# RWKV attention with a two-layer MLP: new planner costs, new load order, no 4-byte loads, filler matmuls

## The chip, the cores and the metric

One core of one Trainium2 chip runs the kernel. The metric is the device time in microseconds (us); the median of the runs is compared.

## What is computed

```python
def _attn_ref(r, k, v, w, u):          # r, k, v: (4, 8, 768, 48); w, u: (8, 48)
    for t in range(S):
        cur = np.einsum('bhd,bhe->bhde', u[None] * kt, vt)
        y[:, :, t] = np.einsum('bhd,bhde->bhe', rt, state + cur)
        state = w[None, :, :, None] * state + np.einsum('bhd,bhe->bhde', kt, vt)

def _moe_ref(x, w_in, w_out):          # x: (3072, 384); d_ff 2048
    h = x @ w_in
    g = np.where(h >= 1, h, np.where(h <= -1, 0.0, (h + 1) ** 2 / 4))
    return g @ w_out                   # x is y with heads and head_dim side by side
```

## The kernel before

The sequence is cut into 6 chunks of 128 steps. Batch b and chunk c make one of 24 **units** (4 batches inside each chunk, so units 0 to 3 have no earlier state). Two units make one of 12 **blocks** of 256 tokens for the MLP.

Attention of a unit: load K, R, V (192 KB each, `add_load`); scale K by `Winv` and R by `Wpow` into a bf16 tile `KR` (`kw`, `rw`); cast V (`v`); transpose `KR` into `RK`; multiply pairs of heads into scores (`at`, L429), mask them into `AT` on DVE (`mask`, L435); read out with `AT` and the state `Tbd` into y (`y`, L485 and L488); add the diagonal term `VD` (`x`, L500); transpose x into `xT`; update the state (`st` on PE L536, `t`, `tw`, `bd`). Units 0 to 7 are **soft**: transposes go through PE (`tr` L409, `xp` L510) and the diagonal through PE (`dg` L451). Units 8 to 23 are hard: both transposes are DMAs on SP's queue (L418, L518) and the diagonal is made by POOL (`ku` L464 and L465, `vd` L475) and DVE.

MLP of a block: 8 groups of layer 1 (`h`, L574: 6 matmuls of 256 columns each), a square on ACT after each (`g`, L586), then 8 groups of layer 2 (`o`, L597: 4 matmuls of 384 columns; 4 groups for each unit), a copy of PSUM (`os`, L242) and a store (`out`, L611). Group n of layer 1 needs quarter n//2 of `w_in`; group s of layer 2 needs quarter s of `w_out`. All eight quarters (768 KB, "I0" to "I3" and "O0" to "O3") are loaded as float32 and cast by ACT, DVE or POOL.

Order of the work. `Plan.run` is a list scheduler in Python that runs when the kernel is built: it keeps a model time for each engine, takes the ready operation with the smallest `due`, picks its engine from the costs (`pe`, `act`, `dve`, `pool`), and writes the result out as fixed in-order queues for the engines. MLP groups are due at 1000 and up, so any ready attention operation goes ahead of them. A DMA's model is a begin at least 0.3 us behind its issue, a given length, and 1.7 us until it counts as landed. `D_m` holds the blocks' due times, `ORDER` the order of the first loads. All loads, stores and DMA transposes stand in SP's one queue; the loads of `w` and `u` stand in ACT's: `w_bc`, `u_bc` and four loads of single 4-byte words into `wraw` and `uraw` (`tiny`), from which `wc` (the decay of a chunk) and `uw` are made.

Of the kernel before, what the change touches and what calls it, by code (L numbers as in the profile page):

```python
# [8 lines left out]
F32 = mybir.dt.float32  # L9
# [116 lines left out]
def pe(t):  # L126
    return {"PE": (t, t + 0.17)}
# [22 lines left out]
def kernel(  # L150
# [11 lines left out]
    nc = tc.nc  # L162
# [16 lines left out]
    NS = 8  # L179
# [12 lines left out]
    P = Plan(slots)  # L192

# [11 lines left out]
    def row_bcast(src):  # L205
        return bass.AP(tensor=src.tensor, offset=src.offset, ap=[[0, 128], [1, H * D]])
# [3 lines left out]
    wraw = const.tile([128, NP], F32, name="wraw")  # L210
    uraw = const.tile([128, NP], F32, name="uraw")
# [36 lines left out]
    def tiny(dst, src):  # L248
        with nc.allow_non_contiguous_dma(reason="384 words"):
# [3 lines left out]
    c_wbc = P.op("c_wbc", {"ACT": (0.6, 2.5)}, lambda e: nc.scalar.dma_start(out=w_bc, in_=row_bcast(w)), due=-100)  # L253
# [7 lines left out]
    kr0 = [P.op(f"c_kr{i}", {"DVE": (0.35, 0.4)}, f_kr(i), due=-90 + i if i < 2 else 0) for i in range(slots["KR"])]  # L261

# [3 lines left out]
    c_icol = P.op("c_icol", {"DVE": (0.3, 0.35)}, f_col, deps=[c_cols], due=-99)  # L266
# [14 lines left out]
    c_wu0 = P.op("c_wu0", {"DVE": (0.3, 0.3)}, f_wu, due=-95)

    def f_wu1(e):
        tiny(wraw, w)
        tiny(uraw, u)
    c_wu = P.op("c_wu", {"ACT": (1.8, 4.0)}, f_wu1, deps=[c_wu0], due=-99)
    c_ubc = P.op("c_ubc", {"ACT": (0.6, 4.5)}, lambda e: nc.scalar.dma_start(out=u_bc, in_=row_bcast(u)), due=-94)
# [54 lines left out]
    w_in_ready = {}  # L342
    w_out_ready = {}
    for q in range(NQ):
        bf = Buf("wf")

        def fn(e, bf=bf, q=q):
            t = get(bf, [128, nKb, FQ], F32)
            nc.sync.dma_start(out=t, in_=w_in_src[:, :, q * FQ : (q + 1) * FQ])

        o = P.op(f"ldI{q}", {"SP": (0.2, 0)}, fn, allocs=[bf], due=-200.0 + pos[f"I{q}"], dma=2.05)
        lst = []
        for kk in range(nKb):
            def fc(e, bf=bf, q=q, kk=kk):
                copy(e, w_in_sb[:, kk, q * FQ : (q + 1) * FQ], bf.t[:, kk, :])
            lst.append(P.op(f"cI{q}{kk}", {**dve(FQ, True), **act(FQ, False), **pool(FQ, False)}, fc, deps=[o], uses=[bf], due=D_m[0] + 1.3 * q))
        w_in_ready[q] = lst
    for q in range(NQ):
        bf = Buf("wf")

        def fn(e, bf=bf, q=q):
            t = get(bf, [128, TQ, d_out], F32)
            nc.sync.dma_start(out=t, in_=w_out_src[:, q * TQ : (q + 1) * TQ, :])

        o = P.op(f"ldO{q}", {"SP": (0.2, 0)}, fn, allocs=[bf], due=-200.0 + pos[f"O{q}"], dma=2.05)
        lst = []
        for i in range(TQ):
            def fc(e, bf=bf, q=q, i=i):
                copy(e, w_out_sb[:, q * TQ + i, :], bf.t[:, i, :])
            lst.append(P.op(f"cO{q}{i}", {**dve(d_out, True), **act(d_out, False), **pool(d_out, False)}, fc, deps=[o], uses=[bf], due=34.0 + 1.0 * q))  # L370
        w_out_ready[q] = lst
# [6 lines left out]
    def attention(i):  # L378
# [16 lines left out]
        o_rw = P.op(f"rw{i}", both, f_rw, deps=[Ro, c_wpow, o_kw], uses=[Rb, krb], due=D0 - 5.8)  # L395
# [4 lines left out]
        o_v = P.op(f"v{i}", {**dve(384, True), **act(384, False), **pool(384, False)}, f_v, deps=[Vo], uses=[Vb], allocs=[vb], due=D0 - 4)  # L400
# [14 lines left out]
        else:  # L415
# [3 lines left out]
            o_rk = P.op(f"trd{i}", {"SP": (1.7, 0)}, f_trd, deps=[o_kw, o_rw], uses=[krb], allocs=[rkb], due=D0 - 9, dma=1.4)  # L419
# [109 lines left out]
        if c < NCH - 1:  # L529
# [203 lines left out]
```

## Time and profile before

| what | value |
|---|---|
| runs (median of 3) | 194.84 us (194.29 to 196.55) |
| the profiled execution | 196.34 us |
| its span, first to last instruction | 194.4 us |
| PE, DVE, ACT, POOL busy | 164.1, 110.5, 107.9, 106.8 us |
| DMA moved | 31.68 MB |

Times in the rows are counted from the span's start. PE's busy time overlaps: a row of x6 matmuls lasts until its last result is out, while the next row has begun. What a group costs PE in a stream is the distance from its start to the next row's start.

### The profile page before, as it was taken

How to read it: one execution, taken by the hardware profiler on the slowest of the kernel's cores; microseconds unless marked ns; L12 is line 12 of the kernel's file. 1: busy time of each engine (PE TensorE's matmuls, PEld its weight loads, DVE VectorE, ACT ScalarE, POOL GpSimd, SP SyncE). 2: the span in 40 equal slices, each digit the busy share in tenths (PEclk: the TensorE clock that was granted, in tenths of full speed). 3: DMA queues.
4: the chain of work that ended last, by engine and by line, in shares of the span. 5: the costliest groups of instructions: out<-in, count | busy, mean ns of one | idle time of the engine just before them, and what ended most of it. 6: DMA issues, size and time to landing. Idle time of an engine off the chain costs nothing.

```text
span 194.4 us, 4322 instructions
## 1 busy us (share of the span) xinstructions
PE 164.1 (84%) x1642; PEld 121.0 (62%) x1642; DVE 110.5 (57%) x223; ACT 107.9 (55%) x226; POOL 106.8 (55%) x155
## 2 busy tenths in 40 slices
PE   0453984988999997998997989799979999999990
PEld 0242873757777766775774767576757777777650
DVE  4669698799999957675556676586845300000000
ACT  2316573785856582866556665645665455555210
POOL 7336163567799895988769797977963000000000
PEclk9999998599999999999999999999999999999998
DMA  5999999989899968898797988888776211111121
GB/s 93 183 302 233 350 180 249 269 204 235 206 233 150 215 130 186 171 199 166 147 208 154 201 179 153 203 183 181 155 159 193 66 42 40 43 41 40 44 82 51
DMA packets 106747, 31.68 MB, mean 163 GB/s; under 512 B 99808, under 2 KB 105184, under 8 KB 106720
## 3 DMA queue, kind: packets, MB, share of 16 engines
q1 hardware_dynamic: 105600, 30.94, 70.5%
q10 hardware_dynamic: 1120, 0.40, 1.4%
q8 instruction: 15, 0.25, 0.6%
q14 instruction: 12, 0.10, 0.2%
HBM read 20.84 MB, written 4.72 MB: 131 GB/s over the span
## 4 chain that ended last, share of the span: by engine, by line
PE 45%; DMA 20%; DVE 12%; POOL 8%; SPq 6%; ACT 4%; issue 3%; DVEq 0%; POOLq 0%; ACTq 0%
PE h L574 19%; PE o L597 19%; DMA Vf<-in_v_dram 7%; DMA R<-in_r_dram 6%; DVE AT L435 4%; DMA K<-in_k_dram 4%; SPq L326 4%; DMA out_dram<-os 3%; PE a L409 2%; POOL VD L475 2%; POOL KR L394 2%; POOL KU L465 2%; DVE x L500 2%; POOL KU L464 1%; PE a L488 1%
## 5 line engine op out<-in xcount | busy, mean ns | idle before, releaser
L574 PE MATMUL h<-xT,w_in_sb 128*128 128x256 bf16 x576 | 79.6, 277 | 2.4 <-ACT g L586 1.9
L597 PE MATMUL o<-w_out_sb,g 128*128 128x384 bf16 x384 | 75.7, 326 | 1.3 <-DVE os L242 1.3
L586 ACT ACTIVATE g<-h 128x512 bf16<-128x512 f32 x96 | 56.0, 593 | 32.0 <-PE h L574 30.7
L574 PEld LDWEIGHTS <-w_in_sb 128*128 128x128 bf16 x576 | 55.2, 99 | 16.6 <-issue 3.1
L597 PEld LDWEIGHTS <-g 128*128 128x128 bf16 x384 | 35.7, 98 | 17.7 <-issue 1.4
L435 DVE TENSOR_TENSOR AT<-a,umask 128x512 bf16<-128x512 f32 x48 | 30.8, 682 | 6.5 <-PE a L429 6.3
L526 ACT ACTIVATE x<-x 128x384 bf16<-128x384 bf16 x24 | 12.5, 522 | 16.8 <-DVE x L500 16.7
L394 POOL TENSOR_TENSOR KR<-R,Wpow 128x384 bf16<-128x384 f32 x16 | 16.6, 1039 | 6.7 <-DMA R<-in_r_dram 5.5
L500 DVE TENSOR_TENSOR x<-a,VD 128x384 bf16<-128x384 f32 x24 | 13.3, 552 | 8.9 <-PE a L488 8.4
L465 POOL TENSOR_TENSOR KU<-KU,R 128x384 f32<-128x384 f32 x16 | 17.1, 1071 | 1.3
L464 POOL TENSOR_TENSOR KU<-K,u_bc 128x384 f32<-128x384 f32 x16 | 17.2, 1076 | 0.0
L475 POOL TENSOR_TENSOR VD<-V,dg 128x384 f32<-128x384 bf16 x16 | 13.6, 855 | 6.6 <-DVE dg L470 3.2
L390 DVE TENSOR_TENSOR KR<-K,Winv 128x384 bf16<-128x384 f32 x16 | 11.3, 709 | 9.1 <-DMA K<-in_k_dram 6.0
L409 PE MATMUL a<-ident,KR 128*128 128x128 bf16 x64 | 6.9, 264 | 8.0 <-DVE KR L390 6.5
L242 ACT COPY os<-o 128x384 f32<-128x384 f32 x16 | 7.6, 478 | 9.3 <-PE o L597 7.1
L242 ACT CAST V<-Vf 128x384 bf16<-128x384 f32 x15 | 7.6, 508 | 8.4 <-DMA Vf<-in_v_dram 8.3
L543 DVE TENSOR_TENSOR T<-T,a 48x192 f32<-48x192 f32 x32 | 11.1, 347 | 1.0 <-PE a L536 0.6
L429 PE MATMUL a<-RK 48*128 48x128 bf16 x192 | 10.4, 229 | 1.5 <-DVE RK L242 1.1
L536 PE MATMUL a<-V,KR 128*128 128x96 bf16 x80 | 7.3, 219 | 5.0 <-ACT V L242 2.6
L409 PEld LDWEIGHTS <-KR 128*128 128x128 bf16 x64 | 5.3, 118 | 8.9 <-DVE KR L390 6.5
L488 PE MATMUL a<-V,AT 128*128 128x48 bf16 x192 | 9.2, 189 | 1.5 <-DVE VD L457 1.3
L536 PEld LDWEIGHTS <-KR 128*128 128x128 bf16 x80 | 5.6, 105 | 6.6 <-issue 6.2
(70 smaller groups left out, 165.9 us busy)
## 6 DMA issues: line engine op xcount, KB each, us to landing
K<-in_k_dram SPq DMA_DIRECT2D x24, 192.0 KB, 4.3
R<-in_r_dram SPq DMA_DIRECT2D x24, 192.0 KB, 3.8
Vf<-in_v_dram SPq DMA_DIRECT2D x24, 192.0 KB, 4.3
out_dram<-os SPq DMA_DIRECT2D x24, 192.0 KB, 2.3
wf<-in_moe_w_in_dram SPq DMA_DIRECT2D x4, 768.0 KB, 7.0
wf<-in_moe_w_out_dram SPq DMA_DIRECT2D x4, 768.0 KB, 6.0
RK<-KR SPq DMA_TRANSPOSE x16, 3.3
xT<-x SPq DMA_TRANSPOSE x16, 2.4
```

The costliest lines, as they stand in the source:

```text
L242: (nc.scalar.copy if eng == "ACT" else V_ENG[eng].tensor_copy)(o, i)
L394: V_ENG[e].tensor_mul(krb.t[:, :H, 0:D], Rb.t, Wpow)
L409: nc.tensor.transpose(trb.t[:, p, :], pair(krb.t, p), ident)
L435: nc.vector.tensor_mul(atb.t[s], at_p[s].t, umask4)
L464: nc.gpsimd.tensor_mul(kub.t, Kb.t, u3)
L465: nc.gpsimd.tensor_mul(kub.t, kub.t, Rb.t)
L475: nc.gpsimd.tensor_mul(vdb.t, vb.t, dgb.t[:, :, None].to_broadcast([128, H, D]))
L500: nc.vector.tensor_add(xb.t, yb.t[:, 0:384].rearrange("p (h d) -> p h d", h=H), vdb.t)
L536: mm(stb.t[:, p, :], pair(krb.t[:, H:, :], p), pair(vb.t, p), start=True, stop=True)
L574: mm(hb.t[:, f, :], w_in_sb[:, kk, (2 * n + f) * 128 : (2 * n + f + 1) * 128], xT[m][:, kk, :], start=(kk == 0), stop=(kk == nKb - 1),)
L586: nc.scalar.activation(gb[m].t[:, 2 * n : 2 * n + 2, :], hb.t, AF.Square, bias=0.5, scale=0.5)
L597: mm(ob.t, gb[m].t[:, f, j * C : (j + 1) * C], w_out_sb[:, f, :], start=(f == 0), stop=(f == nN - 1))
```

## The change

The planner gets a new DMA model: each DMA has a length, a number of descriptors and a start delay; an issuing queue holds at most 160 descriptors in its ring; only 8 DMAs of SP and ACT are in flight; a DMA counts as landed 0.6 us behind its end (1.6 us after model time 45). After 45 each PE operation of attention is taken to be ready 0.6 us later than its inputs. Due times, the loads' order and the stores' due time change. In hard units `rw` is on DVE alone, `v` on ACT alone, `bd` on ACT alone; in soft units `bd` is on ACT or POOL. The four 4-byte loads go: `wc` and `uw` are made from one row by 8 small transposes on PE. `u_bc` moves from ACT's queue to SP's, behind unit 7. Matmuls of a zero tile into a spare bank fill PE's planned idle time until model time 24; 224 of them are left in the program.

```diff
+CFG = {
+    "order": "U0 U1 U2 U3 I0 I1 I2 I3 O0 O1 U4 O2 O3 U5 U6 U7",
+    "soft": 8, "sw": False, "due": [13.0, 22.0, 30.0, 36.0, 42.0],
+    "step": 12.6, "warm": 24.0, "steady": 45.0,
+}
...
+                if o.dma and "POOL" not in o.engs and len(lanes) >= 8:
+                    ready = max(ready, lanes[-8])
+                if "PE" in o.engs and ready > steady and o.name[0] != "L":
+                    ready += 0.6
+                if o.late is not None and max(free["PE"], ready) > o.late:
+                    gone.append(o)
+                    continue
...
-                issue = est + occ
-                if len(dmas) >= 2:
-                    issue = max(issue, dmas[-2])
-                begin = max(dma_end, issue + 0.3)
-                dma_end = begin + o.dma
-                dmas.append(dma_end)
+                took, nd, wait = o.dma
+                issue, ring = est + occ, rings[e]
+                while sum(n for t, n in ring if t > issue) + nd > 160:
+                    issue = min(t for t, n in ring if t > issue)
+                begin = max(served, issue + wait)
+                served = begin + took
+                ring.append((served, nd))
                 free[e] = issue
-                o.end = dma_end + 1.7
+                o.end = served + 0.6 + (1.0 if est > steady else 0.0)
...
-    def tiny(dst, src):
-            for s in range(2):
-                nc.scalar.dma_start(out=dst[halves[s], :], in_=src.rearrange("(p s) d -> s d p", s=2)[s])
+    c_ur = P.op("c_ur", {"ACT": (0.4, 0)}, lambda e: nc.scalar.dma_start(out=u_row, in_=...), after=[c_wbc], ...)
+    c_ubc = P.op("c_ubc", {"SP": (0.4, 0)}, lambda e: nc.sync.dma_start(out=u_bc, in_=row_bcast(u)), ...)
...
+    def f_z(e):
+        nc.vector.memset(zero, 0.0)
+        nc.vector.memset(ones, 1.0)
+        nc.vector.memset(onef, 1.0)
+        nc.vector.memset(rows, 0.0)
+        nc.vector.memset(uw, 0.0)
...
+    def f_colT(e):
+        get(colb, [128, 2, NP], F32)
+        for i in range(2):
+            for p in range(NP):
+                nc.tensor.transpose(colb.t[:, i, p : p + 1], rows[:, i, 2 * p : 2 * p + 2, :].rearrange("q h d -> q (h d)"), onef)
...
+    for i in range(160):
+        def f_wm(e, i=i):
+            for _ in range(2):
+                mm(wmb.t, zero, zero, start=True, stop=True, skip_group_check=True)
+        wm0 = P.op(f"wm{i}", pe(0.11), f_wm, deps=[c_z], ..., due=2000.0, late=CFG["warm"] if i else None)
...
-    D_m = [13.0, 18.0, 24.0, 30.0, 36.0] + [44.0 + 12.4 * i for i in range(NB)]
...
-        o_rw = P.op(f"rw{i}", both, f_rw, ...)
+        o_rw = P.op(f"rw{i}", both if soft else {"DVE": both["DVE"]}, f_rw, ...)
-        o_v = P.op(f"v{i}", {**dve(384, True), **act(384, False), **pool(384, False)}, f_v, ...)
+        o_v = P.op(f"v{i}", {**act(384, False), **({**dve(384, True), **pool(384, False)} if soft else {})}, f_v, ...)
-            o_bd = P.op(f"bd{i}", {**scaled(act(192, False), 2), **scaled(pool(192, False), 2), **scaled(dve(192, True), 2)}, f_bd, ...)
+            o_bd = P.op(f"bd{i}", {**scaled(act(192, False), 2), **(scaled(pool(192, False), 2) if soft else {})}, f_bd, ...)
-        P.op(f"out{i}", {"SP": (0.4, 0)}, ..., due=lambda ready, last: ready + 2, dma=0.5)
+        P.op(f"out{i}", {"SP": (0.4, 0)}, ..., due=lambda ready, last: oe.end - 12, dma=(0.8, 8, 0.6))
```

SP's queue, the first loads before. `wf` is a quarter of a weight, K, R and Vf one unit each; the rows begin with unit 1.

```order
L326 DMA K_148<-in_k_dram 128x8x48
L326 DMA R_151<-in_r_dram 128x8x48
L326 DMA Vf_154<-in_v_dram 128x8x48
L349 DMA wf_159<-in_moe_w_in_dram 128x3x512
L349 DMA wf_179<-in_moe_w_in_dram 128x3x512
L326 DMA K_188<-in_k_dram 128x8x48
L326 DMA R_215<-in_r_dram 128x8x48
L326 DMA Vf_262<-in_v_dram 128x8x48
L349 DMA wf_273<-in_moe_w_in_dram 128x3x512
L349 DMA wf_282<-in_moe_w_in_dram 128x3x512
L326 DMA K_297<-in_k_dram 128x8x48
```

The same queue now, from unit 3 on.

```order
L366 DMA K_359<-in_k_dram 128x8x48
L366 DMA R_389<-in_r_dram 128x8x48
L366 DMA Vf_424<-in_v_dram 128x8x48
L402 DMA wf_452<-in_moe_w_in_dram 128x3x512
L402 DMA wf_474<-in_moe_w_in_dram 128x3x512
L402 DMA wf_491<-in_moe_w_in_dram 128x3x512
L402 DMA wf_510<-in_moe_w_in_dram 128x3x512
L402 DMA wf_535<-in_moe_w_out_dram 128x4x384
L366 DMA K_554<-in_k_dram 128x8x48
L402 DMA wf_629<-in_moe_w_out_dram 128x4x384
L366 DMA R_676<-in_r_dram 128x8x48
L366 DMA Vf_747<-in_v_dram 128x8x48
```

Before, two quarters came behind unit 1, two behind unit 2, and one behind each of units 4 to 7. Now all of `w_in` and half of `w_out` come between units 3 and 4, and the other two quarters behind unit 4.

PE's queue around its first layer-1 group, before (repeated rows left out; L510 is `xp` of unit 1, L409 `tr` of unit 2):

```order
L510 LDWEIGHTS x_301
L510 MATMUL a_305<-ident,x_301 128x128
L574 LDWEIGHTS w_in_sb
L574 MATMUL h_315<-xT_94,w_in_sb 128x256
L409 LDWEIGHTS KR_84
L409 MATMUL a_327<-ident,KR_84 128x128
```

The same place now (L469 is `at` of unit 3, L338 a filler, L491 `dg` of unit 3):

```order
L469 LDWEIGHTS RK_542
L469 MATMUL a_589<-RK_542 128x128
L338 LDWEIGHTS zero
L338 MATMUL o_131<-zero 128x128
L614 LDWEIGHTS w_in_sb
L614 MATMUL h_620<-xT_96,w_in_sb 128x256
L491 LDWEIGHTS P_601
L491 MATMUL a_631<-uw,P_601 128x2
```

Layer 1 of block 0 stood behind the attention of units 0 and 1; now it stands behind nearly all PE work of units 0 to 3. 96 fillers stand ahead of PE's first transpose, 2 right ahead of it and 126 between later attention operations.

## Rows read from the trace of the kernel before

**Rows 1.** The page: busy time, share and instructions of each engine.

```profile
PE 164.1 (84%) x1642; PEld 121.0 (62%) x1642; DVE 110.5 (57%) x223; ACT 107.9 (55%) x226; POOL 106.8 (55%) x155
```

**Rows 2.** Busy time by stretch (us): columns as the first line says.

```profile
core 0: us, PE busy (x) PEld busy (x) DVE busy (x) ACT busy (x) POOL busy (x), PEclk, DMA share, GB/s
0.00:19.36 19.36, 6.62 (x71) 4.52 (x72) 13.02 (x30) 7.18 (x15) 9.81 (x28) 1.00 0.88 202
19.36:31.59 12.23, 9.60 (x108) 7.83 (x107) 10.24 (x21) 6.44 (x14) 4.83 (x8) 1.00 0.99 266
31.59:39.23 7.64, 6.86 (x71) 5.33 (x71) 5.50 (x12) 5.49 (x11) 3.69 (x6) 0.55 1.01 246
39.23:48.00 8.77, 7.31 (x96) 5.43 (x93) 8.23 (x16) 6.68 (x16) 6.45 (x11) 1.00 0.93 214
48.00:60.00 12.00, 11.52 (x134) 9.09 (x132) 11.23 (x23) 7.81 (x18) 10.62 (x14) 1.00 1.05 226
60.00:150.00 90.00, 82.73 (x886) 60.76 (x885) 60.29 (x119) 55.28 (x121) 71.43 (x92) 1.00 0.86 176
150.00:189.50 39.50, 39.47 (x294) 28.00 (x289) 1.98 (x6) 18.53 (x34) 0.00 (x0) 1.00 0.14 49
```

**Rows 3.** Timeline of PE, 6 to 22 us: start, us, what, idle before.

```profile
6.54 0.61 PE L409 MATMUL a<-ident,KR 128*128 128x128 bf16 x4 [6.54 <-DVE KR L390]
...
19.36 1.44 PE L574 MATMUL h<-xT,w_in_sb 128*128 128x256 bf16 x6 [0.57 <-ACT xT L242]
20.59 1.06 PE L409 MATMUL a<-ident,KR 128*128 128x128 bf16 x8
21.44 0.53 PE L536 MATMUL a<-V,KR 128*128 128x96 bf16 x4
```

**Rows 4.** Timeline of PE, 46 to 51 us.

```profile
46.05 0.82 PE L574 MATMUL h<-xT,w_in_sb 128*128 128x256 bf16 x6
46.80 0.40 PE L429 MATMUL a<-RK 48*128 48x128 bf16 x8
47.13 0.25 PE L451 MATMUL a<-uw,P 128*128 128x2 bf16 x4
47.24 0.81 PE L597 MATMUL o<-w_out_sb,g 128*128 128x384 bf16 x4
47.89 1.47 PE L574 MATMUL h<-xT,w_in_sb 128*128 128x256 bf16 x12
49.20 0.61 PE L409 MATMUL a<-ident,KR 128*128 128x128 bf16 x8
49.65 0.34 PE L485 MATMUL a<-Tbd,RK 128*128 128x96 bf16 x4
49.82 0.36 PE L488 MATMUL a<-V,AT 128*128 128x48 bf16 x8
50.02 0.33 PE L536 MATMUL a<-V,KR 128*128 128x96 bf16 x4
```

**Rows 5.** Timeline of ACT: two operations released by loads.

```profile
12.47 0.51 ACT L242 CAST V<-Vf 128x384 bf16<-128x384 f32 x1 [4.00 <-DMA Vf<-in_v_dram]
...
50.73 0.93 ACT L242 CAST w_out_sb<-wf 128x384 bf16<-128x384 f32 x2 [0.73 <-DMA wf<-in_moe_w_out_dram]
```

**Rows 6.** Waits of SP's queue: who, for whom, us in total, times, longest.

```profile
SPq L611 <- ACT os L242: 34.9, 10, 4.9
...
SPq L326 <- DMA K<-in_k_dram: 1.1, 1, 1.1
```

**Rows 7.** Groups by line, 60 to 150 us.

```profile
L242 ACT CAST Tbd<-T 48x192 bf16<-48x192 f32 x16 | 5.6, 348 | 1.4 <-POOL T L548 1.1
```

**Rows 8.** Timeline of DVE: its zeroing of KR, and what follows it.

```profile
1.40 2.11 DVE L258 MEMSET KR<- 128x512 uint32 x4
5.93 0.56 DVE L390 TENSOR_TENSOR KR<-K,Winv 128x384 bf16<-128x384 f32 x1 [2.42 <-ACT Winv L290]
```

**Rows 9.** Timeline of PE: the last readout of attention (unit 23).

```profile
149.77 0.36 PE L488 MATMUL a<-V,AT 128*128 128x48 bf16 x8
```

More of the change, by code (lines that the diff above doesn't have):

```diff
@@ L15 @@
 SEM = 0.06
+CFG = {
+    "order": "U0 U1 U2 U3 I0 I1 I2 I3 O0 O1 U4 O2 O3 U5 U6 U7",
+    "soft": 8,
+    "sw": False,
+    "due": [13.0, 22.0, 30.0, 36.0, 42.0],
+    "step": 12.6,
+    "warm": 24.0,
+    "steady": 45.0,
+}
 class Buf:
@@ L23, with __init__ @@
 class Op:
-    def __init__(self, name, engs, fn, deps, uses, allocs, due, dma, after, nb):
+    def __init__(self, name, engs, fn, deps, uses, allocs, due, dma, after, nb, late):
         self.name, self.engs, self.fn, self.due, self.dma = name, engs, fn, due, dma
-        self.after, self.nb = [a for a in after if a], nb
+        self.after, self.nb, self.late = [a for a in after if a], nb, late
         self.deps, self.uses, self.allocs = [d for d in deps if d], list(uses), list(allocs)
@@ L66, in run @@
     def run(self):
-        free = dict.fromkeys(("PE", "ACT", "DVE", "POOL", "SP", "ACTQ"), 0.0)
-        dmas, dma_end = [], 0.0
+        free = dict.fromkeys(("PE", "ACT", "DVE", "POOL", "SP"), 0.8)
+        rings = {"SP": [], "ACT": [], "POOL": []}
+        lanes, served = [], 2.1
         todo, done, last_mlp = list(self.ops), [], "L2"
+        steady = CFG["steady"]
         while todo:
-            cand = []
+            cand, gone = [], []
             for o in todo:
                 if any(d.start is None for d in o.deps) or any(a.start is None for a in o.after):
+                    if o.late is not None and free["PE"] > o.late:
+                        gone.append(o)
                     continue
@@ L78, in run @@
                 ready = max([d.end + SEM for d in o.deps] + [a.start + 0.001 for a in o.after] + [pl[0], o.nb])
+                if o.dma and "POOL" not in o.engs and len(lanes) >= 8:
[3 more added lines that the diff above has]
+                if o.late is not None and max(free["PE"], ready) > o.late:
+                    gone.append(o)
+                    continue
                 for e in o.engs:
                     cand.append((max(free[e], ready), ready, o, e, pl[1]))
-            if not cand:
+            for o in gone:
+                todo.remove(o)
+                for b in o.uses:
+                    b.users.remove(o)
+            if not cand and not todo:
+                break
                 raise RuntimeError("no operation can be placed: " + ", ".join(o.name for o in todo[:12]))
@@ L178 @@
     LIM = 0.95
-    NS = 8
+    NS = CFG["soft"]
+    D_m = list(CFG["due"])
+    while len(D_m) < NB + 2:
+        D_m.append(D_m[-1] + CFG["step"])
     mm = nc.tensor.matmul
@@ L192 @@
     P = Plan(slots)
+    rows = rot.tile([1, 2, H, DP], F32, name="rows", tag=f"g_{slots['g'] - 1}")
     def get(b, shape, dtype):
@@ L259, in f_kr @@
         return fn
-    kr0 = [P.op(f"c_kr{i}", {"DVE": (0.35, 0.4)}, f_kr(i), due=-90 + i if i < 2 else 0) for i in range(slots["KR"])]
+    kr0 = [P.op(f"c_kr{i}", {"DVE": (0.48, 0.5)}, f_kr(i), due=-90 + i) for i in range(slots["KR"])]
     def f_col(e):
@@ L275, with f_uw @@
     c_um = P.op("c_um", {"POOL": (0.6, 0.7)}, f_um, due=-97)
-    def f_wu(e):
-        nc.vector.memset(wraw, 1.0)
-        nc.vector.memset(uraw, 1.0)
+    def f_z(e):
+        nc.vector.memset(zero, 0.0)
         nc.vector.memset(ones, 1.0)
[L281 to L287, printed above, removed]
+        nc.vector.memset(onef, 1.0)
+        nc.vector.memset(rows, 0.0)
+        nc.vector.memset(uw, 0.0)
+    c_z = P.op("c_z", {"DVE": (0.5, 0.5)}, f_z, due=-95)
+    c_lrow = P.op("c_lrow", act(384, False), lambda e: nc.scalar.activation(rows[:, 0, :, 0:D], w_bc[0:1].rearrange("p (h d) -> p h d", h=H), AF.Ln), deps=[c_wbc, c_z], due=10)
+    c_urow = P.op("c_urow", dve(384), lambda e: nc.vector.tensor_mul(rows[:, 1, :, 0:D], w_bc[0:1].rearrange("p (h d) -> p h d", h=H), u_row.rearrange("p (h d) -> p h d", h=H)), deps=[c_wbc, c_ur, c_z], due=8.5)
+    colb = Buf("a")
+    def f_colT(e):
[3 more added lines that the diff above has]
+                nc.tensor.transpose(colb.t[:, i, p : p + 1], rows[:, i, 2 * p : 2 * p + 2, :].rearrange("q h d -> q (h d)"), onef)
+    c_colT = P.op("c_colT", pe(0.5), f_colT, deps=[c_lrow, c_urow], allocs=[colb], due=9)
+    c_wc = P.op("c_wc", {"ACT": (0.15, 0.2)}, lambda e: nc.scalar.activation(wc, colb.t[:, 0, :], AF.Exp, scale=float(C)), deps=[c_colT], uses=[colb], due=10)
+    def f_uw(e):
+        for s in range(2):
+            nc.vector.tensor_copy(uw[halves[s], :, s], colb.t[halves[s], 1, :])
+    c_uw = P.op("c_uw", {"DVE": (0.3, 0.35)}, f_uw, deps=[c_colT, c_z], uses=[colb], due=9)
+    wmb = Buf("o")
+    for i in range(160):
+        def f_wm(e, i=i):
+            if wmb.t is None:
+                get(wmb, [128, 128], F32)
+            for _ in range(2):
+                mm(wmb.t, zero, zero, start=True, stop=True, skip_group_check=True)
+        wm0 = P.op(f"wm{i}", pe(0.11), f_wm, deps=[c_z], uses=[wmb] if i else [], allocs=[] if i else [wmb], after=[wm0] if i else [], due=2000.0, late=CFG["warm"] if i else None)
     flat = lambda t: t.rearrange("p h d -> p (h d)")
@@ L343 @@
-    w_out_ready = {}
-    for q in range(NQ):
+    w_in_ready, w_out_ready = {}, {}
+    prev_w = []
+    for tag, q in [(x[0], int(x[1:])) for x in ORDER if x[0] in "IO"]:
         bf = Buf("wf")
[L347 to L371, printed above, removed]
+        if tag == "I":
+            src, dst, shape = w_in_src[:, :, q * FQ : (q + 1) * FQ], w_in_sb[:, :, q * FQ : (q + 1) * FQ], [128, nKb, FQ]
+        else:
+            src, dst, shape = w_out_src[:, q * TQ : (q + 1) * TQ, :], w_out_sb[:, q * TQ : (q + 1) * TQ, :], [128, TQ, d_out]
@@ new lines, with fn, fc @@
+        nd = 24 if tag == "I" else 32
+        res = w_in_ready if tag == "I" else w_out_ready
+        due = -200.0 + pos[f"{tag}{q}"]
+        before = ORDER[: pos[f"{tag}{q}"]]
+        gate = [loads[int(x[1:])]["Vf"][1] for x in before if x[0] == "U"][-1:]
+        if CFG["sw"]:
+            def fn(e, src=src, dst=dst):
+                nc.gpsimd.dma_start(out=dst, in_=src)
+            o = P.op(f"ld{tag}{q}", {"POOL": (1.1, 0)}, fn, after=gate + prev_w[-1:], due=due, dma=(2.05, 0, 1.0))
+            res[q] = [o]
+        else:
+            def fn(e, bf=bf, src=src, shape=shape):
+                t = get(bf, shape, F32)
+                nc.sync.dma_start(out=t, in_=src)
+            o = P.op(f"ld{tag}{q}", {"SP": (0.6, 0)}, fn, allocs=[bf], due=due, dma=(2.05, nd, 0.6))
+            res[q] = []
+            for i in range(shape[1]):
+                def fc(e, bf=bf, dst=dst, i=i):
+                    copy(e, dst[:, i, :], bf.t[:, i, :])
+                n = shape[2]
+                due_c = D_m[0] + 1.3 * q if tag == "I" else 34.0 + 1.0 * q
+                res[q].append(P.op(f"c{tag}{q}{i}", {**dve(n, True), **act(n, False), **pool(n, False)}, fc, deps=[o], uses=[bf], due=due_c))
@@ L374 @@
+        prev_w.append(o)
     state = {}
```

49 lines of the change are left out of this document (21 added, 28 removed).

## The prediction

> **What bounds the kernel now.** I read the busy line first, then a table of busy time by stretch, then PE's timeline in the first 50 us, and last the waits of SP's queue. PE is the busiest engine with 164.1 of 194.4 us, and no other is over 111 [rows 1]. So the question is where PE is not doing useful work. The table by stretch answers it [rows 2]: in the first 19.36 us PE is busy for 6.62; from 19.36 to 48 it is busy for 9.60 + 6.86 + 7.31 = 23.77 of 28.64; from 60 to 150 for 82.73 of 90; from 150 to 189.5 without a gap; and the 4.9 us behind that, up to 194.4, are the last copy, the last store and the end of the program.
>
> Busy is not yet useful. The price of each group at full rate is the distance between starts in a dense stretch [rows 4]: `h` 0.655 us (two from 47.89 to 49.20), `o` 0.65 (47.24 to 47.89), `tr` 0.45, `at` 0.33, `y` 0.20 and `yT` (L485) 0.17, `dg` 0.11; for `st` and `xp` I take 0.17 from the like-sized `yT`. Early groups cost double. The first `h` starts at 19.36 and the next row at 20.59, 1.23 us later, and eight transposes take from 20.59 to 21.44, 106 ns each [rows 3], against 56 ns from 49.20 to 49.65 [rows 4]. [...] Between 31.59 and 39.23 the granted clock itself is 0.55, with PE busy for 6.86 us [rows 2], so about half of that, 3.4 us, is lost.
>
> Now count useful work in program order. A soft unit costs 0.45 + 0.33 + 0.20 + 0.17 + 0.11 + 0.17 = 1.43 us, or 1.60 with `yT`; a hard one 0.87; the MLP is 96 x 0.655 + 96 x 0.65 = 125.3. The program needs about 152 us of PE; the 42 us beyond that are the 4.9 at the end and some 37 of gaps and half-rate work. By 47.89 us PE has done 14 `h`, 3 `o`, units 0 to 5 and most of unit 6: 9.2 + 1.95 + 10.0 = 21.1 us. At 50.5 us it stands at about 23.8.
>
> **The loads' order.** This is the main part. The transfers keep the DMA engines full from 19 us to 60 (share 0.93 to 1.05) [rows 2], so their order decides what PE can do. The V of unit 1 is there at 12.45 us and O3 at 50.7 [rows 5]: between them stand 18 loads of 192 KB (units 2 to 7) and 8 quarters, 38.25 us. The stretches move 202 to 266 GB/s [rows 2]; those with mostly loads, 202 and 226, give 192 KB in 0.97 and 0.87 us, and I take 0.95; then a quarter costs (38.25 - 17.1) / 8 = 2.64 us. The change moves the same bytes. Unit 1 should be there sooner, at about 10.5: SP waited 1.1 us for the first K before it could issue a fourth load [rows 6], and the four 4-byte loads are gone from the front. From there: unit 3 complete at 16.2, I0 18.8, I1 21.5, I2 24.1, I3 26.8, O0 29.4, K of unit 4 at 30.4, O1 33.0, unit 4 at 34.9, O2 37.5, O3 40.2, units 5, 6 and 7 at 43.0, 45.9 and 48.7.
>
> I follow PE's new queue through these times, with 1.0 us for the casts of a quarter and 1.0 for `rw` ahead of a transpose. The first `h` comes at about 20, but with units 0 to 2 and most of 3 behind it (before: 0 and 1). The last `h` of block 0 ends at 28.9 (I3), the first `o` at 31.0 (O0), `tr` of unit 4 at 35.7 (its R), the third `o` at 39.2 (O2), the fourth at 41.8 (O3), `tr` of unit 5 at 43.7, of unit 6 at 46.8; between these the queue holds enough `h` and `o` to fill PE. At 50.5 us it has done 17 `h`, 12 `o` and the same attention (units 0 to 5 and most of 6): 11.1 + 7.8 + 10.0 = 28.9. That is 5.1 us more than before. It contains most of what the half-rate stretch cost, since the replay is at full clock. Bounds: nothing, if the clock falls again (3.4) and DVE's casts come late (1.7); 8 if PE also fills the waits that I left at 33 to 47. I take 5.1.
>
> **4-byte loads.** In their place come one row load, one Ln and one multiply of 384 elements on one partition, 8 transposes with one column and three small operations. DVE gets 1024 words to zero, about 1.06 us by its zeroing of KR (2.11 / 4 = 0.53 for 512 words); it sat idle for 2.42 us before its first multiply [rows 8], which hides it. Their gain is the earlier unit 1 above; it lies ahead of I0 and is worth at most the 1.1 us of [rows 6], bounds -0.5 to 1.6, and stands in the 5.1.
>
> **Fillers.** 98 of them stand ahead of the first transpose. At 106 ns [rows 3] they would take 10.4 us, at 56 ns [rows 4] 5.5; they can start at about 1 us. PE's first transpose came at 6.54, waiting for KR [rows 3]. So they end between 6.5 and 11.4; I take 8.5 (the clock rises part-way). A delay of 2 us to unit 0 is covered, as PE waits for I0 until 18.8. The other 126 (7.1 us at 56 ns) lie in waits. Cost taken: 0; bounds 0 to 3 us.
>
> [...]
>
> **Engines in the hard units and the 0.6 us.** From the order: POOL loses a net 5 multiplies of KR and 6 `bd`, DVE gets a net 5 multiplies, ACT gets 8 `bd` (2 x 0.348 us each [rows 7]), 3 copies of RK, 2 V and 2 `os`: about 11 us over the whole program. In the steady stretch ACT is busy for 55.28 of 90, POOL for 71.43 [rows 2], so work goes from the fuller to the emptier. PE's attention operations stand later behind their inputs. PE's gaps from 60 to 150 are 90 - 82.73 = 7.3 us; I expect some 5.5 of them to stay. Gain 1.8; bounds -7 (ACT's additions fall in front of `g`, on which PE waits) and 6.
>
> **Stores** stand further ahead in SP's queue. SP waited 34.9 us for copies of `os`, in 10 waits [rows 6]; I take them to lie in the stretch of pure MLP, where no load is behind them. Cost 0; the third rival has the other end.
>
> **Sum.** 194.4 - 5.1 - 1.8 = 187.5 us of span. The profiled execution took 196.34 us, 1.94 more than its span, so such an execution would take 189.4; the median of the runs shown, 194.84, is 1.5 below it, so I predict 194.84 - 6.9 = 187.9 us. As a check on the other side: in program order the last `y` now has 16 `h` and 21 `o` behind it (24 us) where it had 23 and 37 (39 us). For an end of PE at 182.6, with 1 to 2 us lost behind it, that `y` may come as late as 157; in the profile it came at 149.8 [rows 9]. So attention isn't asked to be faster than it was.
>
> **Rivals.**
> 1. Fillers in the way, or the clock falls again. [...] One more stretch like that of 31.59 to 39.23 costs 3.4. Either ends near 191. For it: PE still has waits of over 1 us at 33 to 47. Against: these hold 85% of useful work in my replay.
> 2. The gain is given back in the steady stretch: PE works with less MLP in reserve behind each attention operation (24 instead of 39 us at the end), and ACT's 11 us delay `g`. If the gaps double from 7.3 to 14, the end is at 194.4 - 5.1 + 6.7 = 196.0 of span, or with 5 us more of gaps 194.3: no change, 194.5 on the scale of the median. For it: ACT's share rises from 61% to about 70%. Against: it stays below POOL's 79% of before.
> 3. Slower: stores hold the loads. A store in SP's in-order queue waits for its `o`, and the K, R, V and DMA transposes behind it wait too; then attention is late, PE waits for it, the next `o` is later. SP's longest wait of this kind is 4.9 us [rows 6]. The last `y` came at 149.8 us, 99 us behind O3's landing at 50.7 [rows 5, 9], near which unit 8's loads begin: 12.4 us for each of the 8 blocks. With 24 us of MLP, 2 of gaps and 4.9 behind the last `y`, the span passes 196.8 when that `y` is later than 166, so from 14.4 us a block on; at 14.7 the end is at 199.
>
> **Chances.** The forecast (183 to 191.5 by itself) 0.60; rival 1 at 191, 0.15; rival 2 at 194.5, 0.13; rival 3 at 199, 0.12. Rival 1 is still over 1% faster, so faster 0.75, the same 0.13, slower 0.12; 1% is about what a measurement of this kernel can tell from no change. The range leaves out rival 3 and the lowest of the forecast: 182 to 195.5.
>
> **What would show it.** Right: the first `h` at 19 to 21 us, at 0.65 us a group; block 1's layer 1 done by about 39 (before 49); no stretch with a granted clock near half after 22 us; 28 to 30 us of useful PE work at 50.5; PE's gaps from 60 to the last `y` between 4 and 7 us. Rival 1 shows as a first transpose behind 10 us or a granted clock near 0.5; rival 2 as waits of `h` on `g` above the gaps of before; rival 3 as SP waiting for `os` in mid-program and PE for RK or xT. I am wrong altogether if unit 3 lands behind 19 us: then everything from I0 on is late by the same.

## The result, and the profile after

The changed kernel takes 186.08 us (median of 3, 185.96 to 186.31) against 194.84 (194.29 to 196.55): 0.953 of before, 95% interval 0.944 to 0.963. Its profiled execution took 186.08 us, with a span of 184.3, 10.1 less than before. Six later runs of the same kernel gave 184.39 (183.36 to 186.16; the control below), so a difference of less than about 2 us between two medians can be scatter.

The page's busy line, the changed kernel, against [rows 1]:

```profile
PE 172.0 (93%) x1874; PEld 131.0 (71%) x1874; DVE 107.4 (58%) x223; ACT 115.1 (62%) x244; POOL 102.3 (56%) x139
```

The 224 fillers are in PE's time, so PE's share says less than before. The table of busy time by stretch (columns as in [rows 2]) says where the 10.1 us are:

```profile
28.00:39.00 11.00, 10.01 (x95) 7.73 (x96) 6.77 (x15) 7.60 (x16) 3.69 (x7) 1.00 0.94 266
39.00:50.50 11.50, 10.12 (x119) 6.61 (x118) 8.97 (x19) 6.73 (x17) 8.37 (x12) 1.00 1.03 174
50.50:60.00 9.50, 9.09 (x112) 7.00 (x111) 8.53 (x18) 6.63 (x16) 7.71 (x9) 1.00 1.02 218
60.00:100.00 40.00, 40.00 (x426) 29.85 (x423) 26.21 (x53) 29.86 (x66) 32.94 (x42) 1.00 1.05 177
100.00:150.00 50.00, 47.46 (x489) 34.57 (x486) 31.24 (x62) 33.66 (x75) 35.24 (x40) 1.00 1.06 185
150.00:179.20 29.20, 29.20 (x242) 21.14 (x240) 3.98 (x10) 14.55 (x28) 0.00 (x0) 1.00 0.15 49
```

From 60 to 150 us PE now idles for 90 - 87.46 = 2.54 us, where it idled for 7.3 [rows 2]: 4.7 us. The granted clock is 1.00 in every row; the half-rate stretch of [rows 2] is gone.

The first 50 us, PE's timeline of the changed kernel:

```profile
0.99 7.55 PE L338 MATMUL o<-zero 128*128 128x128 bf16 x96 [0.99 <-DVE zero L308]
9.18 0.61 PE L449 MATMUL a<-ident,KR 128*128 128x128 bf16 x8
...
22.30 0.82 PE L614 MATMUL h<-xT,w_in_sb 128*128 128x256 bf16 x6
...
31.36 0.81 PE L637 MATMUL o<-w_out_sb,g 128*128 128x384 bf16 x4 [0.57 <-POOL w_out_sb L275]
...
50.35 0.81 PE L614 MATMUL h<-xT,w_in_sb 128*128 128x256 bf16 x6
```

The row at 50.35 is the 17th `h`. Ahead of it stand 16 `h`, 12 `o` and attention up to unit 6: 10.5 + 7.8 + 10.0 = 28.3 us of useful work by the prediction's prices, where there were 23.8. That is 4.5 us. With the 4.7 of the later stretch this makes 9.2 of the 10.1; the rest lies in half microseconds that I don't place.

POOL's timeline shows when loads land, as POOL waits for most of them (idle time and releaser in brackets):

```profile
11.82 0.50 POOL L275 CAST V<-Vf 128x384 bf16<-128x384 f32 x1 [0.87 <-DMA Vf<-in_v_dram]
...
18.51 0.50 POOL L275 CAST V<-Vf 128x384 bf16<-128x384 f32 x1 [1.03 <-DMA Vf<-in_v_dram]
20.51 0.61 POOL L275 CAST w_in_sb<-wf 128x512 bf16<-128x512 f32 x1 [1.50 <-DMA wf<-in_moe_w_in_dram]
22.56 0.61 POOL L275 CAST w_in_sb<-wf 128x512 bf16<-128x512 f32 x1 [1.43 <-DMA wf<-in_moe_w_in_dram]
...
30.04 1.27 POOL L275 CAST w_out_sb<-wf 128x384 bf16<-128x384 f32 x2 [1.70 <-DMA wf<-in_moe_w_out_dram]
33.09 0.69 POOL L275 CAST w_out_sb<-wf 128x384 bf16<-128x384 f32 x1 [1.78 <-DMA wf<-in_moe_w_out_dram]
37.62 1.08 POOL L275 CAST w_out_sb<-wf 128x384 bf16<-128x384 f32 x2 [3.83 <-DMA wf<-in_moe_w_out_dram]
39.86 0.95 POOL L275 CAST w_out_sb<-wf 128x384 bf16<-128x384 f32 x2 [0.69 <-DMA wf<-in_moe_w_out_dram]
```

Unit 1 came at 11.8 (predicted 10.5), unit 3 at 18.5 (16.2), I0 and I1 at 20.5 and 22.6 (18.8, 21.5), O0 to O3 at 30.0, 33.1, 37.6 and 39.9 (29.4, 33.0, 37.5, 40.2). Quarters in a row came every 2.05 us, not every 2.64; the six loads of units 2 and 3 took 6.7 us, 1.1 apiece and not 0.95.

PE's waits between 60 and 150 us say what its 7.3 us of gaps were before (who waits for whom: us in total, times, longest):

```profile
PE h L574 <- ACT g L586: 1.9, 2, 1.2
PE a L536 <- DVE V L242: 1.6, 2, 1.3
PE o L597 <- DVE os L242: 1.3, 1, 1.3
PE a L536 <- ACT V L242: 1.2, 2, 0.9
PE a L536 <- POOL V L242: 0.8, 1, 0.8
```

Half of them, 3.6 us, is the state update waiting for a cast of V. In the changed kernel no wait for V is left there; its 2.5 us are waits for RK (1.1), and of `h` (0.9) and `o` (0.5) for `g`.

### The profile page after: what moved, and what is told of

It is laid out like the page before. It is cut to its first block, busy times and chain, and to the rows that moved or that the text cites. A ratio compares the mean times of both kernels' runs of the same rounds, so it can differ in the third digit from the quotient of the medians.

```text
span 184.3 us, 4816 instructions
## 1 busy us (share of the span) xinstructions
PE 172.0 (93%) x1874; PEld 131.0 (71%) x1874; DVE 107.4 (58%) x223; ACT 115.1 (62%) x244; POOL 102.3 (56%) x139
## 4 chain that ended last, share of the span: by engine, by line
PE 51%; DMA 20%; SPq 19%; DVE 2%; ACT 2%; issue 1%; POOL 1%; ACTq 0%
PE o L637 23%; PE h L614 22%; SPq L366 15%; DMA wf<-in_moe_w_out_dram 7%; DMA RK<-KR 5%; DMA K<-in_k_dram 5%; DMA R<-in_r_dram 3%; SPq L402 3%; PE a L469 2%; PE a L525 1%; PE a L528 1%; ACT g L626 1%; PE a L576 1%; POOL w_out_sb L275 1%; DVE AT L475 1%
## 5 line engine op out<-in xcount | busy, mean ns | idle before, releaser
L614 PE MATMUL h<-xT,w_in_sb 128*128 128x256 bf16 x576 | 77.8, 272 | 1.4 <-ACT g L626 0.9
L637 PE MATMUL o<-w_out_sb,g 128*128 128x384 bf16 x384 | 77.3, 326 | 1.2 <-POOL w_out_sb L275 0.6
L504 POOL TENSOR_TENSOR KU<-K,u_bc 128x384 f32<-128x384 f32 x16 | 19.4, 1209 | 7.1 <-DMA K<-in_k_dram 7.1
L338 PE MATMUL o<-zero 128*128 128x128 bf16 x224 | 17.3, 236 | 1.0 <-DVE zero L308 1.0
L430 POOL TENSOR_TENSOR KR<-K,Winv 128x384 bf16<-128x384 f32 x13 | 13.0, 998 | 6.5 <-DMA K<-in_k_dram 5.1
L338 PEld LDWEIGHTS <-zero 128*128 128x128 bf16 x224 | 14.9, 107 | 1.4 <-DVE zero L308 1.0
L434 DVE TENSOR_TENSOR KR<-R,Wpow 128x384 bf16<-128x384 f32 x18 | 13.2, 732 | 3.3 <-DMA R<-in_r_dram 3.2
L275 ACT CAST Tbd<-T 48x192 bf16<-48x192 f32 x34 | 11.8, 347 | 1.3 <-PE a L525 0.5
L510 DVE TENSOR_REDUCE dg<-KU 128x8 f32<-128x384 f32 x16 | 8.7, 546 | 5.8 <-POOL KU L505 5.8
L469 PE MATMUL a<-RK 48*128 48x128 bf16 x192 | 9.5, 219 | 1.1 <-DMA RK<-KR 1.1
L430 DVE TENSOR_TENSOR KR<-K,Winv 128x384 bf16<-128x384 f32 x11 | 6.4, 583 | 7.1 <-DMA K<-in_k_dram 6.3
```

What stands on the lines that cost most here:

```text
L275: (nc.scalar.copy if eng == "ACT" else V_ENG[eng].tensor_copy)(o, i)
L338: mm(wmb.t, zero, zero, start=True, stop=True, skip_group_check=True)
L430: V_ENG[e].tensor_mul(krb.t[:, H:, 0:D], Kb.t, Winv)
L504: nc.gpsimd.tensor_mul(kub.t, Kb.t, u3)
L614: mm(hb.t[:, f, :], w_in_sb[:, kk, (2 * n + f) * 128 : (2 * n + f + 1) * 128], xT[m][:, kk, :], start=(kk == 0), stop=(kk == nKb - 1),)
L637: mm(ob.t, gb[m].t[:, f, j * C : (j + 1) * C], w_out_sb[:, f, :], start=(f == 0), stop=(f == nN - 1))
```

## The experiments

Theory A is the prediction's: the gain is the order of the loads, with what it does to the clock, and a steadier stretch behind it. Rivals put it into the fillers and the clock (B), the later readiness of PE's operations (C), the fixed engines (D), or the 4-byte loads. The runs stand in three groups, each with its own runs of the kernel before (medians 195.93, 195.75 and 195.95 us); a ratio is to those, with its 95% interval. Edits are to the changed kernel where nothing else is said. Windows have the columns of [rows 2].

**Fillers planned, not issued** (the only computation left out anywhere; no output depends on it).

```diff
-            for _ in range(2):
+            for _ in range(0):
                 mm(wmb.t, zero, zero, start=True, stop=True, skip_group_check=True)
```

> The changed kernel with the 224 filler matmuls planned but not issued; every other instruction stands where it stood. [...] If the clock is the main gain (theory B), half-rate work and a second stretch near half clock come back: 190 us or more.

186.02 us, 0.947 (0.940 to 0.955): nothing lost, where theory B asked for 190 or more. PE's timeline without fillers:

```profile
21.29 1.46 PE L614 MATMUL h<-xT,w_in_sb 128*128 128x256 bf16 x6
...
22.70 1.44 PE L614 MATMUL h<-xT,w_in_sb 128*128 128x256 bf16 x6
...
24.89 1.47 PE L614 MATMUL h<-xT,w_in_sb 128*128 128x256 bf16 x12
```

The first two `h` run at half rate (1.46 and 1.44 us for 6 matmuls), but the first starts 1.0 us sooner, and from 24.89 the rate is full (12 matmuls in 1.47). Block 1's layer 1 ends at 38.6, with fillers at 38.8. So in this run PE came to full rate without fillers, between 22.70 and 24.89; what brought it there isn't shown. The loads came sooner, too; POOL's timeline:

```profile
16.61 0.50 POOL L275 CAST V<-Vf 128x384 bf16<-128x384 f32 x1
18.59 0.61 POOL L275 CAST w_in_sb<-wf 128x512 bf16<-128x512 f32 x1 [1.48 <-DMA wf<-in_moe_w_in_dram]
```

Unit 3 and I0 were there 1.9 us ahead of the changed kernel's 18.51 and 20.51, close to the 16.2 and 18.8 predicted. In the nine profiled runs with fillers and w_in right behind unit 3, POOL's first cast of a weight began between 19.7 and 21.1. So the fillers seem to hold the first loads back; by what path isn't shown.

**The old order of loads, with the new planner.**

```diff
-    "order": "U0 U1 U2 U3 I0 I1 I2 I3 O0 O1 U4 O2 O3 U5 U6 U7",
+    "order": "U0 U1 I0 I1 U2 I2 I3 U3 U4 O0 U5 O1 U6 O2 U7 O3",
```

> The changed kernel with the loads' order of before (U0 U1 I0 I1 U2 I2 I3 U3 U4 O0 U5 O1 U6 O2 U7 O3), all else kept. Theory A: most of the first part's 5 us goes, 190 to 192 us, with block 1's layer 1 ending 4 us or more later than 38.8. Theory B: 186 to 188 us.

191.23 us; three of four runs at 191.0 to 192.1, one at 186.36, so no interval is given. The one at 186.36 is as fast as the changed kernel and left no trace, so this experiment alone doesn't fix the order's price; the new order in the kernel before (two further on) has no such run. Windows of the profiled execution (span 189.2):

```profile
28.00:39.00 11.00, 7.18 (x76) 4.80 (x75) 8.65 (x16) 4.09 (x10) 6.91 (x12) 0.72 1.06 236
...
60.00:100.00 40.00, 40.00 (x405) 28.93 (x403) 27.19 (x53) 26.93 (x62) 33.31 (x40) 1.00 1.11 184
100.00:150.00 50.00, 47.96 (x490) 34.75 (x489) 31.42 (x62) 33.78 (x76) 37.98 (x44) 1.00 1.07 178
```

The half-clock stretch is back (0.72 over 28 to 39, PE idle for 3.8 us), while the steady stretch is as full as in the changed kernel (2.04 us idle against 2.54). So in this execution the 4.9 us between the spans are lost ahead of 60 us: close to the prediction's load-order term, 5.1, by itself. Counted as above, PE has done 23.9 us of useful work at 50.5.

**The same, with fillers until 45**, meant to hold the clock where the old order leaves PE waiting (0.72 over 28 to 39, above). To the edit above comes:

```diff
-    "warm": 24.0,
+    "warm": 45.0,
```

> The changed kernel with the loads' order of before and fillers planned until model time 45 instead of 24. It tells how the order's 5 us are made up: if most of it is the stretch near half clock at 33 to 40 us that comes back with the old order, and fillers can hold the clock there, 187 to 188.5 us; if PE waits for the later data anyway, 190 to 192 us, with or without that stretch.

188.79 us, 0.965 (0.954 to 0.977), between the two ranges expected; profiled span 188.0.

```profile
28.00:39.00 11.00, 10.05 (x166) 8.51 (x165) 8.16 (x18) 5.88 (x14) 7.08 (x12) 1.00 0.97 238
```

The clock stays at 1.00 there, and 2.4 us come back by the medians (1.2 by the spans; useful work at 50.5 is 25.2 us against 23.9). The single runs overlap (186.86 to 189.74 against 186.36 to 192.14), so that fillers pay here is likely, not certain. The rest of the order's gain is not the clock: with the new order and no low clock either, useful work at 50.5 is 28.4 us, as the weights are there sooner (POOL casts O0 to O3 from 30.0, 33.1, 37.6 and 39.9 us in the changed kernel, from 34.5, 40.2, 46.4 and 51.5 here).

**The kernel before, with the new order alone.**

```diff
-    ORDER = ["U0", "U1", "I0", "I1", "U2", "I2", "I3", "U3", "U4", "O0", "U5", "O1", "U6", "O2", "U7", "O3"]
+    ORDER = "U0 U1 U2 U3 I0 I1 I2 I3 O0 O1 U4 O2 O3 U5 U6 U7".split()
```

> The kernel before with one change, the new loads' order (U0 U1 U2 U3 I0 I1 I2 I3 O0 O1 U4 O2 O3 U5 U6 U7); due times, costs, 4-byte loads as before, no fillers. Theory A (the order carries the first part's gain by itself): 189 to 191 us, no stretch near half clock behind the first layer-1 groups. Rival (the order needs the new model and due times, or the fillers): 193 us or more.

191.58 us, 0.981 (0.970 to 0.992): 4.2 us, a little less than expected (189 to 191 us). All four runs lie between 190.32 and 191.97.

```profile
28.00:39.00 11.00, 9.73 (x105) 7.82 (x103) 8.35 (x19) 8.06 (x17) 3.72 (x7) 1.00 1.00 289
...
60.00:100.00 40.00, 37.77 (x415) 27.53 (x415) 34.17 (x66) 26.27 (x60) 33.64 (x42) 1.00 0.94 184
100.00:150.00 50.00, 46.56 (x484) 34.43 (x482) 34.68 (x66) 31.20 (x67) 38.28 (x48) 1.00 0.80 172
```

Without any filler the half-clock stretch is gone (1.00 over 28 to 39, PE idle for 1.3 us), and useful work at 50.5 is 28.2 us, nearly the changed kernel's 28.4. The steady stretch still has 5.7 us of idle PE, 2.6 of them waits for V: that part belongs to the rest of the change.

**No margin for PE's attention operations:** no 0.6 us of readiness, and a DMA counts as landed 0.6 us behind its end all through.

```diff
-    "steady": 45.0,
+    "steady": 1e9,
```

> The changed kernel without the planner's later readiness in the steady part (no 0.6 us for PE's attention operations, no 1.0 us for landings). If that margin closed PE's gaps from 60 to 150 us (2.5 us of idle time now, 7.3 before; theory C), 3 to 5 us come back: 189 to 191 us. If the gaps closed because the engines of the hard units were fixed or because the MLP runs ahead (theory D): 186 to 187.

187.94 us, 0.957 (0.947 to 0.966): between the two ranges expected, and about 2 us above the run without fillers (186.02) and the next one (185.97), which stand beside it and have the changed kernel's time. The single runs overlap (186.85 to 189.32 against 184.21 to 187.86), so the 2 us are likely, not certain. Little of it lies where the margin was meant to help: from 60 to 150 PE idles for 3.0 us against 2.5. It idles for 1.2 against 0.4 from 50.5 to 60, and for 1.0 against nothing from 150 to 179.2. Which of the two parts carries it stays open.

**Any engine in the hard units again**, for `rw` (shown), `v` and `bd` alike:

```diff
-        o_rw = P.op(f"rw{i}", both if soft else {"DVE": both["DVE"]}, f_rw, ...)
+        o_rw = P.op(f"rw{i}", both, f_rw, ...)
```

> The changed kernel with rw, v and bd of the hard units free to go to any engine, as before. Theory C: 185.5 to 187 us. Theory D (fixed engines closed the gaps): 188 to 191 us, with POOL busier from 60 to 150 and PE waiting for it.

185.97 us, 0.944 (0.933 to 0.955): the same as the changed kernel. Fixing the engines is worth nothing measurable.

**The 4-byte loads back** in ACT's queue; the row load, its Ln, its multiply and the 8 transposes out.

```diff
-    c_colT = P.op("c_colT", pe(0.5), f_colT, deps=[c_lrow, c_urow], allocs=[colb], due=9)
...
+    c_wu = P.op("c_wu", {"ACT": (1.8, 4.0)}, f_wu1, deps=[c_z], due=-99)
```

> The changed kernel with the four 4-byte loads back in place of the row load, its Ln, its product and the 8 small transposes. By my working they cost about a microsecond ahead of unit 1 and nothing behind it: 185.5 to 187.5 us. If they hold up the whole first stage: 188 us or more, with the first layer-1 group behind 23.5 us.

184.24 us, 0.942 (0.931 to 0.954), below the 185.5 expected at best: the first `h` at 21.91 against 22.30, and no loss: taking these loads away was worth nothing that can be measured.

**Unit 4 ahead of O1 in SP's queue.** In the changed kernel SP waits 3.4 us for a weight buffer, ahead of O1; here the unit's loads fill that wait.

```diff
-    "order": "U0 U1 U2 U3 I0 I1 I2 I3 O0 O1 U4 O2 O3 U5 U6 U7",
+    "order": "U0 U1 U2 U3 I0 I1 I2 I3 O0 U4 O1 O2 O3 U5 U6 U7",
```

> The changed kernel with unit 4 ahead of the second quarter of w_out (O0 U4 O1 O2 O3). In the changed kernel's trace SP waits 3.4 us for a free weight buffer ahead of O1, with unit 4 behind it. If that wait matters, 184.5 to 185.5 us; if PE has enough work in hand there, 185.5 to 187 us.

185.68 us, 0.951 (0.941 to 0.961): no change, as expected if PE has work in hand. SP's wait is gone from the trace, and the time is the same: it cost nothing that these runs can tell.

**Control: the changed kernel again**, six runs beside the next three.

> The changed kernel itself, unchanged, as the control beside the next three on one chip: 185.5 to 187 us.

184.39 us, 0.942 (0.937 to 0.947): below the 185.5 to 187 expected, so the kernel's runs scatter more than the three at first showed.

**The old due times.**

```diff
-    "due": [13.0, 22.0, 30.0, 36.0, 42.0],
-    "step": 12.6,
+    "due": [13.0, 18.0, 24.0, 30.0, 36.0, 44.0],
+    "step": 12.4,
```

> The changed kernel with the due times of the blocks as before (13, 18, 24, 30, 36, 44 and 12.4 us a block). The order without the rest gave about 4 of the 9 us, the margin of the steady part about 2. If the due times hold what is left, 188 to 190 us; if they only reorder work of equal urgency, 185.5 to 187.5 us.

188.63 us, 0.965 (0.959 to 0.971), clear of the control. Windows:

```profile
60.00:100.00 40.00, 39.07 (x412) 28.58 (x410) 32.88 (x60) 28.13 (x62) 28.64 (x35) 1.00 0.99 170
100.00:150.00 50.00, 46.65 (x481) 33.64 (x477) 30.82 (x60) 33.29 (x75) 35.28 (x40) 1.00 0.90 188
```

and of the control:

```profile
60.00:100.00 40.00, 39.48 (x419) 29.47 (x417) 27.33 (x53) 29.26 (x65) 33.33 (x42) 1.00 1.06 178
100.00:150.00 50.00, 48.84 (x499) 35.73 (x497) 31.97 (x62) 34.75 (x77) 34.87 (x39) 1.00 1.08 185
```

PE idles for 4.28 us here and for 1.68 in the control. Its waits with the old due times, the first two rows,

```profile
PE h L614 <- ACT g L626: 2.1, 4, 0.9
PE o L637 <- ACT g L626: 1.3, 1, 1.3
```

and in the control, the first row:

```profile
PE h L614 <- ACT g L626: 1.4, 3, 0.7
```

So with the old due times PE waits for `g` for 3.4 us, with the new ones for 1.4: it seems that PE now more often has another operation to do while ACT makes `g`. The due times carry about 4 us by the medians (2.2 by the profiled spans, 186.6 and 184.4; the control's is the longest of its six runs).

**A planner without rings and lanes.**

```diff
-                while sum(n for t, n in ring if t > issue) + nd > 160:
+                while sum(n for t, n in ring if t > issue) + nd > 10**6:
...
-                if o.dma and "POOL" not in o.engs and len(lanes) >= 8:
+                if o.dma and "POOL" not in o.engs and len(lanes) >= 10**6:
```

> The changed kernel with a planner that knows no ring of 160 descriptors and no limit of 8 DMAs in flight. If knowing them places the operations where the data really is, 188 to 191 us with PE waiting for loads and casts before 50 us; if the lengths and the order alone do it, 185.5 to 187.5 us.

209.87 us, 1.070 (1.063 to 1.078): slower than before by 14 us, where 191 was the most expected. This is not the planner of the kernel before: that one had a limit too, as an issue waited there for the end of the DMA before the last (`issue = max(issue, dmas[-2])`). In this plan no limit of the DMA queue holds an issue back. SP's queue from O0 on:

```order
L402 DMA wf_4_351<-in_moe_w_out_dram 128x4x384
L366 DMA K_4_361<-in_k_dram 128x8x48
...
L366 DMA Vf_3_647<-in_v_dram 128x8x48
L402 DMA wf_0_663<-in_moe_w_out_dram 128x4x384
```

O1 has to wait for a free weight buffer. For this planner SP never has to wait for room in its ring, so it places units 4 to 9 in the meantime, 18 loads and `u_bc`; in the changed kernel one load, the K of unit 4, stands between O0 and O1. On the chip O1 waits behind all 19, and SP comes to it at 46.4 us, not at 21.9. Rings and lanes went out together, so which of them matters isn't shown. PE's timeline:

```profile
30.39 0.81 PE L637 MATMUL o<-w_out_sb,g 128*128 128x384 bf16 x4
55.04 0.81 PE L637 MATMUL o<-w_out_sb,g 128*128 128x384 bf16 x4 [0.74 <-DVE w_out_sb L275]
...
66.17 7.31 PE L637 MATMUL o<-w_out_sb,g 128*128 128x384 bf16 x44
```

The second `o` comes 24.7 us behind the first; then layer 2, held back so long, runs as 44 matmuls in a row, and attention is late, as the windows show:

```profile
39.00:50.50 11.50, 9.96 (x113) 8.05 (x114) 9.00 (x19) 7.14 (x16) 6.62 (x9) 0.70 0.92 156
...
60.00:100.00 40.00, 29.50 (x273) 18.64 (x271) 29.13 (x53) 17.33 (x41) 33.79 (x40) 0.96 1.19 190
```

PE idles for 10.5 us from 60 to 100 alone, and the clock falls again at 39 to 50.5, to 0.70.

**4-byte loads and any engine together**, by the edits of those two runs.

> The changed kernel with the 4-byte loads back and the hard units' rw, v and bd free to go to any engine. Each of the two alone was not slower than the changed kernel (184.2 and 186.0 us). If the gain of the 4-byte loads is real and the two add up, 183 to 185 us; if both were scatter, 185.5 to 186.5 us.

184.00 us, 0.938 (0.931 to 0.944). It lies in the range expected for gains that add up, but so does the control's 184.39 beside it: a simpler kernel of the same speed, none faster.

## Why the prediction was right

The time, 186.1, lies 1.8 us below the 187.9 predicted. By its steps:

- **Load order, 5.1 us:** right. 4.5 by counting useful work at 50.5, 4.2 by the new order on the old planner, 4.9 by the old order on the new planner in its profiled execution. Both halves of the reasoning are shown: the half-rate stretch goes with the order alone (1.00 over 28 to 39, with no filler), and weights come sooner (O3 at 39.9 us against 50.7). Inside the term two errors cancel, which is luck: unit 3 was 2.3 us late and the first `h` came at 22.3 instead of 19 to 21, while quarters in a row were faster than 2.64 us (2.05). Unit 3 at 18.5 was close to the 19 us from which on the prediction called itself wrong altogether.
- **Steady stretch, 1.8 us:** the term that was mis-sized. I took the 7.3 us of gaps to shrink to 5.5; they shrank to 2.5, a gain of 4.7. The 2.9 us between explain most of the 3.2 by which the span (184.3) undercut the predicted 187.5. Of the two causes I named, the fuller use of ACT is worth nothing that shows (with any engine allowed, nothing is lost), and PE's operations standing later behind their inputs about 2 us, of which only 0.5 shows in this stretch. The due times, to which the prediction gave no term, are worth about 4 us by the medians and 2.6 us of this stretch's gaps. What ended the 3.6 us of waits for V stays open: with no fillers, no margin, any engine, 4-byte loads, unit 4 early or the old due times, each taken by itself, PE waits for V for at most 0.5 us between 60 and 150. Not tried were the new model of the DMAs against the old one, and the due times of the loads of units 8 to 23, which are now 18 us ahead of their block's and were 16.
- **Planner's ring model:** not priced either. A plan in which no limit of the queue holds issues back is slower than before with the new order and due times. What the new model is worth against the old one's limit wasn't tried.
- **4-byte loads, in the 5.1:** unit 1 was taken to come 1.95 us sooner (12.45 to 10.5), of which [rows 6] gave only 1.1; it came 0.6 us sooner, and the time is the same with the loads back.
- **Fillers, cost 0:** right in the end (186.02 without, 186.08 with), and the first block ended at 8.5, as taken. The reason was not right: the delay to unit 0 was to be covered by the wait for I0, but with fillers I0 itself came 1.9 us later. Early work at half rate and late loads come out equal here. The first `h` ran at full rate behind fillers (0.82 us) and at half rate without (1.46). It did start 1.0 us sooner without the 12 fillers right ahead of it (21.29 against 22.30), but I0 came sooner too, so what those 12 cost isn't shown.
- **Engines:** moved as the order said (ACT 107.9 to 115.1, POOL 106.8 to 102.3), without effect on the end.

The rivals. Fillers in the way or a second fall of the clock: the first transposes came at 9.18, and no row has the clock near half. The gain given back by late `g`: of the changed kernel's waits one such row counts,

```profile
PE h L614 <- ACT g L626: 0.9, 1, 0.9
```

against 1.9 before, so no; with the old due times it comes back in part. Stores that hold loads: SP's own waits show

```profile
SPq L651 <- ACT os L275: 22.1, 6, 4.8
SPq L402 <- POOL w_in_sb L275: 3.4, 1, 3.4
```

6 waits for `os`, 22.1 us against 34.9 [rows 6], all of them behind 150 us, where no load is left: as the prediction took them. Its mechanism, a load that waits in SP's queue behind other DMAs, did show, though, in the run without rings: O1 stood behind 19 DMAs there, and the second `o` came 24.7 us behind the first. Not tried: the stores' due time by itself, and the landing delay by itself. The parts interact (due times were set for this order and this model), so the single worths don't add up to one split.

## What to carry to other kernels

Where an offline planner fixes in-order queues, its model of the DMA queue comes first: a plan that believes issues to be free puts what is needed soon behind what is not, and here this cost 25 us. Then measure due times and margins, not just orders and engines: here the due times moved about 4 us and the margin perhaps 2, the choice of engines nothing that shows. Before adding work to hold a clock, look whether the useful work is late there because its data is; here getting the data there sooner removed both: over 28 to 39 us PE idled for 3.8 us at a clock of 0.72 with the old order, for 1.0 at 1.00 with the new.

## What the runs showed of the hardware

- Behind matmuls of a zero tile PE worked at full rate sooner: 96 of them took 7.55 us, 79 ns apiece, between the 106 of half and the 56 of full rate [rows 3, 4], and the transposes at 9.18 took 0.61 us for 8, as at 49.20 in the kernel before [rows 4]; without fillers the first 8 of `KR` took 1.03 us. The first `h` took 0.82 us with them and 1.46 without.
- The granted clock in the rows read 1.00 while matmuls ran at half rate, in the kernel before until 21 us (106 ns a transpose) [rows 2, 3] and without fillers at 21 to 24 us (1.46 and 1.44 us for 6 matmuls of `h`); there the durations told it, the clock did not. Between 31.59 and 39.23 in the kernel before it did fall, to 0.55 [rows 2].
- The four small loads of 4-byte words at the front cost nothing that the runs can show (184.24, and 184.00 with free engines too; 184.39 without).
- Fillers and later loads: with fillers unit 3 and I0 were there at 18.5 and 20.5 us, in the run without them at 16.6 and 18.6; the path is open.
